# A two-layer kernel with a retention front end: a new list of loads, and another way to transpose two of its chunks

## The chip, the cores and the metric

The kernel runs on one core of a Trainium2 chip. The metric is the device time of one execution in microseconds (us); the median of six runs of the kernel before is 211.2 us (210.93 to 211.39). The core has TensorE (PE in the profile; PEld are its weight loads), VectorE (DVE), ScalarE (ACT), GpSimd (POOL) and SyncE (SP), which here does little but issue transfers. Each engine works through its own instructions in order, and engines meet at semaphores.

## The reference

Inputs q, k and v are float32 of shape 4 batches x 8 heads x 768 positions x 64. The first part is a linear attention with decay, the second a two-layer network with a squared relu; w_in is 512 x 2048 and w_out is 2048 x 512.

```python
gamma = 1.0 - 2.0 ** (-5.0 - np.arange(H))
for t in range(S):
    state = gamma[None, :, None, None] * state + np.einsum('bhd,bhe->bhde', k[:, :, t], v[:, :, t])
    y[:, :, t] = scale * np.einsum('bhd,bhde->bhe', q[:, :, t], state)
x = y.transpose(0, 2, 1, 3).reshape(B * S, H * D)     # 3072 tokens x 512
h = np.maximum(x @ w_in, 0.0)
out = h * h @ w_out                                   # 3072 x 512
```

## The kernel before

**Tiling.** The 3072 tokens are cut into 24 chunks of 128 (six a batch). Chunks 0 to 3 are handled as two pairs (`together`, `pair_visits`), named by their first chunk, pair 0 and pair 2. Each later chunk has a *visit* (`visit`, L714): values and state for chunk m, scores and sums for chunk n = m + 1. The decay is folded into scalings: v is multiplied by `vf` as it is cast to bf16, and the output by `yf` as it is written to `xt`, the input x of the network, transposed. `P` operations mask the scores, `S` operations add up the states, `Y` operations write x.

**Transposes.** The scores need q and k transposed (`qkT`). There are three ways, chosen by chunk number in `transpose` (L639): below NPE (from chunk 4), four 128x128 TensorE transposes each for k and q, and two evacuations; from NPE up to NTD, *flips*, which are 32 64x64 TensorE transposes inside the visit of an earlier chunk, into the bank of `yy`, and one evacuation on ACT (L635); from NTD on, one DMA transpose (`X`, L646), which SP issues. The visit that does the flips of chunk t is the one with n = t - 1, so it waits for the casts of k and q of chunk t as well.

**The network.** The first layer (`ffn1`, L804) works in blocks of 2, 2, 1, 1, 2, 2, 2, 4, 4, 4 chunks. Each group of matmuls fills one PSUM bank, ACT takes the relu (L827) and DVE squares (L832). The second layer (`ffn2`, L847) takes one chunk at a time and adds up in one bank over the four slices of w_out; at most two such accumulations are open at once. Four banks (`fps`) serve both layers and the 128x128 transposes.

**Weights.** w_in comes as i0 to i5: its first two quarters in halves (i0 and i1, i2 and i3, 512 KB each), the others whole (i4, i5, 1 MB). w_out comes as o0 to o3, 1 MB each. All land in float32 in four staging tiles `wst` and are cast to bf16 from there. In `weights` (L785) the tile is chosen by

```python
slot = (j if kind == "in" else 4 + j) % NWS
```

with NWS = 4 and j the quarter, so o0 uses the tile of i0 and i1, o1 that of i2 and i3, o2 that of i4, o3 that of i5, and each waits for the casts of what was there before.

**The order of the work.** Nothing is scheduled on the chip. A planner, `Plan.schedule`, places all operations with modelled lengths, earliest start first and then by priority, and the instructions are written out in that order. It also chooses the engine of an operation that could run on several (casts, evacuations), unless `HOME` names one, and `RANK` replaces a priority. The priority of a load is its place in `ORDER` (L233); loads are issued by SP. For loads the model keeps a ring of 198 outstanding descriptors, the time at which descriptors are made, and a pipe that moves bytes; it also models that TensorE's instructions are fetched in blocks of 256, and that a fetch makes one of the DMA engines late (`late`). TensorE's own priorities: the second layer's by F2LAG, the visits' by PACE, below which they go ahead of all else. Where the model leaves TensorE idle in the first 20 us, it puts in *fills*, matmuls of the identity with itself (L923), whose results are not used. `PRE` is a number of 1x1 matmuls ahead of everything.

Of the kernel before, what the change touches and what calls it, by code (L numbers as in the profile page):

```python
# [18 lines left out]
class Plan:  # L19
# [21 lines left out]
    def add(self, name, eng, dur, reads=(), writes=(), fn=None, prio=0.0, lat=0.0, bank=None, after=(), count=0):  # L41
# [17 lines left out]
        else:  # L59
            flex = True  # L60
        if name in HOME:
            eng = {HOME[name]: eng[HOME[name]]}
        prio = RANK.get(name, prio)
# [4 lines left out]
    def schedule(self, nbanks, max_open):  # L68
        ops = self.ops
        n = len(ops)  # L70
        users = [[] for _ in range(n)]
        left = [len(o["deps"]) for o in ops]
        for o in ops:
            for d in o["deps"]:
                users[d].append(o["i"])
        ready_at = [0.0] * n
        start = [None] * n
        end = [None] * n
        eng_free = {}
        pool = {}  # L80
        for o in ops:
            for e in o["eng"]:
                eng_free.setdefault(e, 0.0)
                pool.setdefault(e, set())
                if left[o["i"]] == 0:
                    pool[e].add(o["i"])
        if "PE" in eng_free:
            eng_free["PE"] = 0.06 * PRE
        bank_free = [0.0] * nbanks
        bank_of = {}  # L90
        open_groups = set()
        closed = {}
        pipe = made = 0.0
        late = []
        outstanding = {e: [] for e in eng_free}
        done = 0
        issued, edge, next_fetched, history, crossed = 2 * PRE, self.BLOCK0, 3.0, [], 0.0
        while done < n:
            best = None
            for eng, cand in pool.items():  # L100
                ef = eng_free[eng]
                for i in cand:
                    o = ops[i]
                    t = max(ef, ready_at[i])
                    b = o["bank"]
                    if b is not None and b[0] == "open":
                        if b[2] and len(open_groups) >= max_open:
                            continue
                        free = [x for x in bank_free if x is not None]
                        if not free:  # L110
                            continue
                        t = max(t, min(free))
                    key = (t, o["prio"], i)
                    if best is None or key < best[0]:
                        best = (key, i, eng)
            assert best is not None, "no operation can be placed"
            (t, _, _), i, eng = best
            o = ops[i]
            for e in o["eng"]:
                pool[e].discard(i)  # L120
            o["on"] = eng
            dur = o["eng"][eng]
            move = isinstance(dur, tuple)
            if move:
                gen, cost, n_desc, hold = dur
                out_ = outstanding[eng]
                while out_ and out_[0][0] <= t:
                    out_.pop(0)
                while sum(x[1] for x in out_) + n_desc > self.RING:
                    t = max(t, out_.pop(0)[0])  # L130
            start[i] = t
            before_open = list(bank_free)
            b = o["bank"]
            if b is not None and b[0] == "open":
                k = min((x, j) for j, x in enumerate(bank_free) if x is not None)[1]
                bank_free[k] = None
                bank_of[b[1]] = k
                if b[2]:
                    open_groups.add(b[1])
            if move:  # L140
                eng_free[eng] = t + hold
                if n_desc:
                    made = max(made, t + self.GEN_LATENCY) + gen
                    ready = made + 0.15
                else:
                    ready = t + hold + 0.5
                pipe = max(max(pipe, t + self.DMA_LATENCY) + cost, ready)
                late = [y for y in (max(max(y, t + self.DMA_LATENCY) + cost, ready) for y in late) if y > pipe + 0.05]
                end[i] = max([pipe] + late) + self.LAND
                out_.append((max([pipe] + late), n_desc))  # L150
                dur = hold
            else:
                if eng == "PE":
                    o["fill"] = 0
                    free = [(x, j) for j, x in enumerate(before_open) if x is not None and x <= max(eng_free[eng], WARM - WARMING)]
                    if WARM - WARMING < t < WARM + 1 and free:
                        o["fill"] = int(max(0.0, t - max(eng_free[eng], WARM - WARMING) - 0.1) / FILL)
                        o["fill_bank"] = min(free)[1]
                    issued += 2 * o["fill"]
                    before = issued  # L160
                    todo, per = 2 * o["count"], dur / max(1, 2 * o["count"])
                    now = t
                    while issued + todo > edge:
                        step = max(0, edge - issued)
                        now = max(now + step * per, next_fetched)
                        issued, todo = max(issued, edge), todo - step
                        ahead = next((y for x, y in reversed(history) if x <= edge - self.AHEAD), 0.0)
                        ahead = max(ahead, crossed)
                        crossed = now
                        edge += self.BLOCK  # L170
                        next_fetched = ahead + min(5.7, max(0.3, pipe - ahead)) + self.FETCH
                    issued += todo
                    dur = now + todo * per - t
                    history.append((issued, t + dur))
                    if any(before < x <= issued for x in range(self.BLOCK0 - self.AHEAD, issued + 1, self.BLOCK)):
                        late.append(max(pipe, t + 0.4) + 1.27)
                    o["dur"] = dur
                eng_free[eng] = t + dur
                end[i] = t + dur + o["lat"]
            if b is not None and b[0] == "close":  # L180
                closed.setdefault(b[1], []).append(end[i])
                if len(closed[b[1]]) == (b[2] if len(b) > 2 else 1):
                    bank_free[bank_of[b[1]]] = max(closed[b[1]])
                    open_groups.discard(b[1])
            if b is not None:
                o["bank_index"] = bank_of[b[1]]
            done += 1
            for u in users[i]:
                same = list(ops[u]["eng"]) == [eng] and not move
                ready_at[u] = max(ready_at[u], start[i] + dur if same else end[i] + self.HOP)  # L190
                left[u] -= 1
                if left[u] == 0:
                    for e in ops[u]["eng"]:
                        pool[e].add(u)
        self.start, self.end, self.on = start, end, [o["on"] for o in ops]
        return sorted(range(n), key=lambda i: (start[i], i))
# [10 lines left out]
WARM = 20.0  # L207
FILL = 0.215
WARMING = 18.4
PACE = 8  # L210
LEAD = 2
NPE = 7
NTD = 8
PRE = 0
WHALF = 2
WHALFD = (0.60, 1.47, 33, 0.6)
CVT = {'DVE': 0.69, 'POOL': 1.3}
TCAST = {'DVE': 0.43, 'ACT': 0.63, 'POOL': 0.78}
TEVAC = {'ACT': 0.6, 'DVE': 0.62}
NPAIR = 2  # L220
F2LAG = 3.0
F2WAIT = 4
LAST = [256, 128, 128]
CAST = {"k": {"DVE": 0.43, "ACT": 0.63, "POOL": 0.78}, "q": {"DVE": 0.43, "ACT": 0.63, "POOL": 0.78}}
# [2 lines left out]
WPRIO = {"in": -2.0, "out": 2.0}  # L227


HOME = {'cwin0.2': 'DVE'}  # L230
ROUND = []
RANK = {}
ORDER = (  # L233
    "q0 k0 v0 i0 k2 q2 v2 i1 i2 i3 k4 v4 i4 q4 i5 o0 k5 o1 q5 o2 v5 o3 k6 q6 v6 k7 q7 v7"
)


# [8 lines left out]
def kernel(  # L246
# [392 lines left out]
    def transpose(m):  # L639


        qkT, t = qkts[m % NQT], kq[m % NBF]
        if m < 2 * NPAIR or NPE <= m < NTD:
            return
        if m >= NPE:
            pl.add(f"X{m}", "SP", TURN, (f"bfk{m % NBF}", f"bfq{m % NBF}"), qkeys(m),  # L646
# [67 lines left out]
    def visit(m, n, t=None):  # L714
# [13 lines left out]
        def fn():  # L728
# [10 lines left out]
            if m is not None:  # L739
                nc.tensor.wait_ge(turn, turns[0])  # L740
                apply(m, 1)
        dur = 0.19 + 0.26 * ((m is not None) + (n is not None) + (t is not None))
        if n is None:
            dur += 0.2
        pl.add(f"V{'' if m is None else m}.{'' if n is None else n}", "PE", dur, reads, writes, fn,
               prio=-300 + n if m is None else -300 + m if m < PACE else (m - LEAD) * 8, lat=0.25,
               count=32 * ((m is not None) + (n is not None) + (t is not None)) + 1)
# [22 lines left out]
        if m is not None:  # L770
            g, u = divmod(m, 4)
            i = where(m)[1]
# [117 lines left out]
    for m in range(-1, NM):  # L890
        n = m + 1
        for x in range(0 if m < 0 else m + AHEAD, min(NM, m + AHEAD + 1)):
            prepare(x)
            transpose(x)
        t = m + 2 if NPE <= m + 2 < NTD else None
        if n < 2 * NPAIR:
# [60 lines left out]
```

## Time and profile before

| | |
|---|---|
| median of six runs | 211.2 us |
| profiled execution | 211.39 us |
| its span, first to last instruction | 209.6 us |
| mean granted TensorE clock | 0.984 |
| TensorE busy | 201.8 us (96%) |
| VectorE, ScalarE, GpSimd busy | 115.9, 87.9, 43.0 us |
| first layer, 640 matmuls (L822) | 93.0 us |
| second layer, 416 matmuls (L867) | 91.6 us |
| fills, 35 matmuls (L923) | 7.1 us |
| moved by DMA | 38.13 MB |
| DMA transposes | 16, each 5.0 us from issue to landing (median) |

Busy times of matmuls overlap, since they are pipelined and their ends are modelled, so the parts add up to more than TensorE's total. A line number names the line of the kernel that made the instruction; casts made through the helper `copy_on` appear under L404 (ACT), L406 (DVE) or L408 (POOL). The rows that issue transfers are marked SPq, and a transfer's own wait appears as "DMA tile<-tensor". Buffer numbers are left out of tile names, and the twin tiles of the pairs are part of `h`.

### The profile page before, as it was taken

The page shows a single profiled execution, that of the slowest core. Times are in us where ns is not written, and L with a number is a line of the kernel's source. Part 1 is how long each engine was busy: PE and PEld are TensorE (multiplying, and loading weights), DVE is VectorE, ACT ScalarE, POOL GpSimd, SP SyncE. Part 2 cuts the span into 40 slices and gives each one's busy share as a digit, 9 for nine tenths or more (in the row PEclk, how much of TensorE's full clock was granted, in tenths as well). Part 3 has the DMA queues.
Part 4 walks back from the last instruction along what each step waited for, and adds up shares of the span by engine and source line. Part 5 has one row for each costly group of instructions (what it writes and reads, how often), then busy time and mean ns, then how long its engine had stood idle before and what let it go on. Part 6 is the DMA issues. An engine that isn't in the chain of part 4 may idle for free.

```text
span 209.6 us, 6038 instructions
## 1 busy us (share of the span) xinstructions
PE 201.8 (96%) x2619; PEld 120.4 (57%) x2619; DVE 115.9 (55%) x252; ACT 87.9 (42%) x148; POOL 43.0 (21%) x71
## 2 busy tenths in 40 slices
PE   6789998999999999999999999999999999999994
PEld 4467886665665878666745444444444444444453
DVE  3667988785574686484825657567554432322100
ACT  8354576443441546234231365323533324534321
POOL 6634243233322121222311224021100000000000
PEclk9966999999999999999999999999999999999999
DMA  6999999999999999999998999999711011011022
GB/s 163 307 300 313 264 368 331 331 269 202 271 190 248 197 203 195 206 161 267 194 245 200 204 209 210 170 213 216 106 60 53 0 58 45 0 50 55 0 100 100
DMA packets 94586, 38.13 MB, mean 182 GB/s; under 512 B 79968, under 2 KB 88544, under 8 KB 94560
## 3 DMA queue, kind: packets, MB, share of 16 engines
q1 hardware_dynamic: 94416, 37.69, 84.0%
q8 instruction: 20, 0.33, 0.7%
q10 hardware_dynamic: 144, 0.07, 0.1%
q14 instruction: 6, 0.05, 0.1%
HBM read 27.26 MB, written 6.29 MB: 160 GB/s over the span
## 4 chain that ended last, share of the span: by engine, by line
PE 78%; DMA 11%; SPq 6%; POOL 1%; ACT 1%; issue 0%; DVE 0%; ACTq 0%
PE fps L867 39%; PE fps L822 33%; DMA qn<-in_q_dram 7%; DMA vn<-in_v_dram 4%; SPq L796 3%; SPq L423 2%; PE yy L673 2%; PE yy L688 1%; PE sc L699 1%; PE sc L710 1%; SPq L603 1%; POOL kqs L408 1%; POOL h L439 1%; ACT qkT L635 0%; PE fps L656 0%
## 5 line engine op out<-in xcount | busy, mean ns | idle before, releaser
L822 PE MATMUL fps<-xt,w_in 128*128 128x256 bf16 (+2 forms) x640 | 93.0, 296 | 0.1
L867 PE MATMUL fps<-w_out,h 128*128 128x512 bf16 (+2 forms) x416 | 91.6, 363 | 0.0
L827 ACT ACTIVATE h<-fps 128x512 bf16<-128x512 f32 x96 | 57.2, 596 | 68.4 <-PE fps L822 66.0
L822 PEld LDWEIGHTS <-w_in 128*128 128x128 bf16 x640 | 57.2, 98 | 30.0 <-issue 0.4
L832 DVE TENSOR_TENSOR h<-h 128x512 bf16<-128x512 bf16 x96 | 42.3, 451 | 47.4 <-ACT h L827 47.2
L867 PEld LDWEIGHTS <-h 128*128 128x128 bf16 x416 | 37.9, 98 | 37.1
L875 ACT ACTIVATE osb<-fps 128x512 f32<-128x512 f32 (+2 forms) x26 | 14.7, 564 | 35.7 <-PE fps L867 35.7
L408 POOL CAST kqs<-kn 128x512 bf16<-128x512 f32 x20 | 12.6, 629 | 48.1 <-DMA kn<-in_k_dram 43.4
L775 DVE TENSOR_TENSOR xt<-yy,yf 128x512 bf16<-128x512 f32 x20 | 13.7, 686 | 15.0 <-PE yy L688 13.9
L408 POOL CAST kqs<-qn 128x512 bf16<-128x512 f32 x20 | 14.2, 712 | 31.8 <-DMA qn<-in_q_dram 31.8
L614 DVE TENSOR_TENSOR vs<-vn,vf 128x512 bf16<-128x512 f32 x20 | 14.4, 718 | 5.8 <-DMA vn<-in_v_dram 5.8
L766 DVE TENSOR_TENSOR state<-sc,state 128x256 bf16<-128x256 f32 x33 | 13.8, 419 | 0.5
L753 DVE TENSOR_TENSOR pt<-sc,cmask 128x512 bf16<-128x512 f32 x20 | 13.6, 681 | 0.3 <-PE sc L710 0.3
L688 PE MATMUL yy<-qkT,state 64*64 64x64 bf16 x296 | 10.0, 198 | 0.2
L923 PE MATMUL fps<-ident 128*128 128x256 bf16 x35 | 7.1, 357 | 1.7 <-POOL ident L339 1.7
L673 PEld LDWEIGHTS <-vs 64*64 64x64 bf16 x320 | 4.2, 107 | 6.7 <-issue 6.6
L688 PEld LDWEIGHTS <-state 64*64 64x64 bf16 x296 | 6.2, 107 | 0.4 <-PE yy L688 0.4
L673 PE MATMUL yy<-pt,vs 64*64 64x64 bf16 x320 | 6.4, 198 | 0.0
L699 PE MATMUL sc<-qkT 64*64 64x64 bf16 x320 | 6.2, 194 | 0.0
L710 PE MATMUL sc<-vs,kqs 64*64 64x64 bf16 x288 | 6.2, 193 | 0.0
L406 DVE CAST w_out<-wst 128x512 bf16<-128x512 f32 x8 | 4.7, 632 | 2.7 <-DMA wst<-in_moe_w_out_dram 2.6
L408 POOL CAST w_in<-wst 128x512 bf16<-128x512 f32 x6 | 4.2, 696 | 8.9 <-DMA wst<-in_moe_w_in_dram 8.9
(65 smaller groups left out, 88.3 us busy)
## 6 DMA issues: line engine op xcount, KB each, us to landing
out_dram<-osb SPq DMA_DIRECT2D x23, 256.0 KB, 2.9
kn<-in_k_dram SPq DMA_DIRECT2D x20, 256.0 KB, 5.0
vn<-in_v_dram SPq DMA_DIRECT2D x20, 256.0 KB, 5.1
qn<-in_q_dram SPq DMA_DIRECT2D x20, 256.0 KB, 4.9
wst<-in_moe_w_out_dram SPq DMA_DIRECT2D x4, 1024.0 KB, 10.5
wst<-in_moe_w_in_dram SPq DMA_DIRECT2D x4, 512.0 KB, 8.5
wst<-in_moe_w_in_dram SPq DMA_DIRECT2D x2, 1024.0 KB, 8.1
qn<-in_q_dram SPq DMA_DIRECT2D x2, 512.0 KB, 6.1
```

The costliest lines, as they stand in the source:

```text
L408: nc.gpsimd.tensor_copy(o, t)
L614: lambda: nc.vector.tensor_tensor(out=o[:], in0=t.rearrange("s (h d) -> s h d", h=H), in1=vf[:, i, :, None].to_broadcast([P, H, D]), op=AL ...
L673: nc.tensor.matmul(yy[L * c : L * c + L, sub, p * L : p * L + L], lhsT=vs[r, 4 * a + j, :], rhs=pt[r, a, j, :], start=(p == 0), stop=True, ...
L688: nc.tensor.matmul(yy[L * c : L * c + L, sub, p * L : p * L + L], lhsT=st[r, j, :], rhs=qkT[r, 1, j, sub * L : sub * L + L], start=False, ...
L753: lambda: nc.vector.tensor_tensor(out=pt[:], in0=sc[:, :, 0:256].rearrange("s g (p t) -> s g p t", p=NJ), in1=cmask[:, None, None, :].to_b ...
L766: f = lambda cc=cc, j1=j1, j0=j0: nc.vector.tensor_tensor(out=sts[j1][:], in0=cc, in1=sts[j0][:], op=ALU.add)
L775: lambda: nc.vector.tensor_tensor(out=xt[:, :, u * C : u * C + C].rearrange("s p (g t) -> s g p t", g=2), in0=yy[:, :, 0:256].rearrange("s ...
L822: nc.tensor.matmul(ps[:, u * n : u * n + n], lhsT=w_in_bf[j][:, cb, c * P : (c + 1) * P], rhs=xt[:, cb, cols], start=(cb == 0), stop=(cb = ...
L827: nc.scalar.activation(h2[:, f0 : f0 + per, cols], ps[:].rearrange("p (u n) -> p u n", u=per), AF.Relu)
L832: nc.vector.tensor_mul(hv, hv, hv)
L867: nc.tensor.matmul(ps[:, 0:w], lhsT=h2[:, fb, u * C : u * C + C], rhs=w_out_bf[j][:, c, ns], start=(fb == 0), stop=(fb == NFB - 1))
L875: lambda o1=o1, slot=slot, ns=ns, w=w: nc.scalar.activation(osbs[slot][:, ns], fps[o1["op"]["bank_index"]][:, 0:w], AF.Copy),
```

## The change

It does four things. In the planner's model of loads, a fetch of instructions is now placed ahead of those loads whose descriptors aren't made yet, and these loads are then made later, with the work that waits for them; before, it went behind the whole pipe. A new `ORDER` puts k0 ahead of q0, loads q and k of the second pair before the first half slice of w_in and v after it, interleaves the slices of w_out with those of w_in, and puts q5, q6 and q7 ahead of k5. NPE goes from 7 to 6 and NTD from 8 to 7: chunk 6 is transposed by flips and no longer by 128x128 transposes, chunk 7 by DMA and no longer by flips. And the constants that the planner works with are others: 20 matmuls of 1x1 at the start, F2LAG 4, PACE 5, a longer modelled visit, an engine named for 27 casts and evacuations, and one evacuation of the first pair put ahead.

```diff
@@ Plan.schedule, a load
+                moves.append((made if n_desc else t, pipe, cost, ready, t, i, out_))
                 pipe = max(max(pipe, t + self.DMA_LATENCY) + cost, ready)
...
-                out_.append((max([pipe] + late), n_desc))
+                out_.append([max([pipe] + late), n_desc, i])
@@ Plan.schedule, a fetch of instructions
-                        late.append(max(pipe, t + 0.4) + 1.27)
+                        behind = [x for x in moves if x[0] > t + 0.4]
+                        y = max(behind[0][1] if behind else pipe, t + 0.4) + 1.27
+                        for _, _, cost, ready, t0, k, out_ in behind:
+                            y = max(max(y, t0 + self.DMA_LATENCY) + cost, ready)
+                            if y + self.LAND > end[k]:
+                                end[k] = y + self.LAND
...
+                                for u in users[k]:
+                                    ready_at[u] = max(ready_at[u], end[k] + self.HOP)
+                        late.append(y)
@@ constants
-PACE = 8
+PACE = 5
-NPE = 7
-NTD = 8
-PRE = 0
+NPE = 6
+NTD = 7
+PRE = 20
-F2LAG = 3.0
+F2LAG = 4.0
-HOME = {'cwin0.2': 'DVE'}
+HOME = {'cq2.1': 'POOL', 'Eq2.0': 'DVE', 'cq0.1': 'ACT', 'cwout3.3': 'ACT', 'cwin2.0': 'DVE', 'cwin0.0': 'ACT', 'ck2.0': 'ACT', 'ck5': 'DVE', 'Eq4': 'DVE', 'Eq0.1': 'ACT', 'cq4': 'ACT', 'cwin1.2': 'ACT', 'ck6': 'DVE', 'Ek0.0': 'DVE', 'cwout2.3': 'DVE', 'cwin1.0': 'ACT', 'cwin3.2': 'DVE', 'Ek4': 'ACT', 'cwout0.3': 'DVE', 'cq0.0': 'DVE', 'ck4': 'POOL', 'cwin5.2': 'ACT', 'cwout0.1': 'DVE', 'cwout3.1': 'DVE', 'cwout1.3': 'DVE', 'cwout1.0': 'DVE', 'cwout0.2': 'DVE'}
-RANK = {}
+RANK = {'Ek0.0': -98.1}
 ORDER = (
-    "q0 k0 v0 i0 k2 q2 v2 i1 i2 i3 k4 v4 i4 q4 i5 o0 k5 o1 q5 o2 v5 o3 k6 q6 v6 k7 q7 v7"
+    "k0 q0 v0 q2 k2 i0 v2 o0 k4 i1 o1 i2 q4 o2 i3 o3 i4 v4 i5 q5 q6 q7 k5 v5 v6 k6 k7 v7"
 )
@@ visit
-        dur = 0.19 + 0.26 * ((m is not None) + (n is not None) + (t is not None))
+        dur = 0.22 + 0.28 * ((m is not None) + (n is not None) + (t is not None))
```

More of the change, by code (lines that the diff above doesn't have):

```diff
@@ L94, in schedule @@
         late = []
+        moves = []
         outstanding = {e: [] for e in eng_free}
@@ L175, in schedule @@
                     if any(before < x <= issued for x in range(self.BLOCK0 - self.AHEAD, issued + 1, self.BLOCK)):
-                        late.append(max(pipe, t + 0.4) + 1.27)
+                        behind = [x for x in moves if x[0] > t + 0.4]
[4 more added lines that the diff above has]
+                                end[k] = y + self.LAND
+                                for x in out_:
+                                    if x[2] == k:
+                                        x[0] = max(x[0], y)
+                                for u in users[k]:
+                                    ready_at[u] = max(ready_at[u], end[k] + self.HOP)
+                        late.append(y)
                     o["dur"] = dur
```

## The prediction

> **What bounds the kernel now.** I read the page first, to see whether TensorE or the transfers set the pace: the row of engines, TensorE's busy tenths, its granted clock, and the transfers' share.
>
> ```profile
> span 209.6 us, 6038 instructions
> PE 201.8 (96%) x2619; PEld 120.4 (57%) x2619; DVE 115.9 (55%) x252; ACT 87.9 (42%) x148; POOL 43.0 (21%) x71
> PE   6789998999999999999999999999999999999994
> PEclk9966999999999999999999999999999999999999
> DMA  6999999999999999999998999999711011011022
> ```
>
> TensorE is full from the tenth slice (47 us) to the tail. The other engines are half idle, and the loads fill the DMA engines long past 50 us. So the change can win or lose only where TensorE waits for data, early. The chain that ended last says the same: ahead of 40 us it runs through loads, after it through matmuls. Four of its rows:
>
> ```profile
> 7.60 8.05 DMA vn<-in_v_dram
> 29.93 9.32 DMA qn<-in_q_dram
> 84.36 0.87 PE fps L822 x8
> 85.23 0.86 PE fps L867 x4
> ```
>
> The last two give the price of a group: 0.87 us for the first layer of a pair (8 matmuls), 0.86 us for the second layer (4 matmuls). The timeline then shows when weights land, by the cast that waits for them, and when TensorE runs dry (columns: start, length, engine, line, operation, and in brackets the idle time before it):
>
> ```profile
> 31.36 2.79 PE L822 MATMUL fps<-xt,w_in 128*128 128x256 bf16 x24
> 34.73 1.05 PE L822 MATMUL fps<-xt,w_in 128*128 128x256 bf16 x8
> 36.28 0.40 PE L656 MATMUL fps<-ident,kqs 128*128 128x128 bf16 x4 [0.50 <-POOL kqs L408]
> ...
> 46.01 1.17 DVE L406 CAST w_out<-wst 128x512 bf16<-128x512 f32 x2 [0.43 <-DMA wst<-in_moe_w_out_dram]
> ...
> 47.10 1.03 PE L867 MATMUL fps<-w_out,h 128*128 128x512 bf16 x4
> ```
>
> Slice o3 of w_out lands at 46.0, its casts end at 47.2. Counting groups from the timeline: by 47.1 all first-layer work of chunks 0 to 4 is done, and of the second layer the six groups that two open accumulations allow without o3. So until 47.1 TensorE uses up whatever lands; behind that stand the ten second-layer groups of chunks 2 to 4 (8.6 us), and it doesn't run dry again. **The last landing of w_out, with what TensorE has finished by then, sets the end.** A second narrow place is chunk 7:
>
> ```profile
> 58.96 2.59 SPq L647 DMA_TRANSPOSE qkT<-kqs  x1
> 65.35 0.32 PE L673 MATMUL yy<-pt,vs 64*64 64x64 bf16 x16
> 66.18 0.69 DVE L775 TENSOR_TENSOR xt<-yy,yf 128x512 bf16<-128x512 f32 x1 [2.58 <-PE yy L688]
> 67.76 1.91 PE L822 MATMUL fps<-xt,w_in 128*128 128x256 bf16 x16
> 76.28 1.90 PE L867 MATMUL fps<-w_out,h 128*128 128x512 bf16 x8
> ```
>
> Chunk 7's x is ready at 66.9 and used at 67.8; only two groups (1.7 us, those at 76.28) were left as other work. TensorE could go without chunks 6 and 7 until 69.5.
>
> **What the Trainium skill says.** "Runtime: NRT & Kernel Launch", Instruction fetch mechanics: instructions arrive in 16 KiB blocks of 256 through the sequencer's own DMA queue. The trace agrees: the instruction queue has 20 packets in 0.33 MB, 16.5 KB each, and 2 x 2619 TensorE instructions are 20.5 blocks. "DMA: Bandwidth & Descriptors", Queues, rings and completion order: all rows share the same 16 engines and take turns. It agrees where it can be seen: slice i1 lands 2.9 us after the transfer ahead of it, its like take 1.5, so a disturbance is worth 1.4 us. "TensorE: Matmul & The Clock Gate", Part 1: half clock until a window of about 3.4 us was busy. Here the clock is 0.50 from 14 to 18 us and 1.00 from 20, and eight 256-column matmuls take 1.92 us at 15.9 but 1.05 at 20.6.
>
> **The change, part by part.**
>
> *List of loads.* Landings now: k0 6.8, v0 8.7, i0 10.2, k2 11.95, q2 13.8, v2 15.7, i1 18.6, i2 20.1, i3 21.9, i4 26.7, i5 30.5, o0 34.25, o1 38.15, o2 42.1, v5 43.2, o3 46.0. Differences price a load: pair 1.85, half w_in slice 1.5, 1 MB slice 2.75, single 1.05. The new list names o0 before i1, but o0 shares a staging tile with i0 and i1 and is issued after their casts; o1 likewise after i2 and i3, o2 after i4, o3 after i5. SP issues what is ready, so I expect: k0 q0 v0 q2 k2 i0 v2 k4 i1 i2 q4 i3 i4 v4 i5 o0 q5 o1 q6 o2 o3, then the rest. Summed with these prices, the same 1.4 us disturbance (put at k4) and 1.0 us (o0 now takes 3.75): k2 12.3, i0 13.8, v2 15.7, k4 18.1, i1 19.6, i2 21.1, i3 23.7, i4 26.4, v4 27.5, i5 30.2, o0 34.0, o1 37.8, o2 41.6, **o3 44.4**. Two single loads stand ahead of o3 in place of three: that is 1.05 of the 1.6 us; the rest is rounding and spacing.
>
> *Half a slice within the second pair.* i0 lands 3.6 us later, at 13.8, cast by 14.5; x of the first pair is ready only at 15.0 (now 14.34+0.69), so nothing waits. In return q2 and k2 land some 1.5 to 1.8 us earlier, so the scores of pair 2 leave the path of v2: its x comes near 20.2 in place of 23.7.
>
> *TensorE, walked through with these landings* (a w_in half's casts 0.7 us, a 1 MB slice's 0.9 to 1.2): first group at 15.0 to 16.9, cold, as now. From 20.3 three groups to 22.9, i2's two to 24.6, i3's two to 26.4, transposes to 26.8, i4's four from 27.3 to 30.8, chunk 4's visits, i5's four to 35.3, chunk 4's four groups (0.89 each) to 38.9, o0's two to 40.6, transposes and o1's two to 42.6, o2's two to 44.6, then a wait for o3's casts until **45.6**. Now the same point is at 47.1: 1.5 us. Against it, the chunk 5 visit (0.37) and one transpose group (0.22) are then still to do, and one pair is gone (next edit): 1.35 us stay.
>
> *Chunk 6 by flips, chunk 7 by DMA transpose.* Two groups of four TensorE transposes leave (0.22 each, from 48.97 for the quartet at 49.05 against its follower at 49.27): 0.44 us, counted above. The 32 flips move from chunk 7 to chunk 6, net zero; two evacuations (0.4 to 0.6 us each on DVE or ACT) leave and the 1.0 us one stays. Added: one DMA transpose, 2.0 to 2.6 us on SP and 4.2 to 6.4 us to landing. Queued behind it on SP are the loads of chunk 8 and stores; those delayed by up to 2.6 us are q8 and v8, and so chunk 8's own transpose, which releases the visit at 65.35. I take 1.0 us of that, as k8 and q8 are 2.5 us apart now[...]; bounds 0 and 2.6. Chunk 7's x then comes near 67.9, and TensorE, ahead by 1.35, has other work until 68.1. Free, just; without that cover, 1 us per us. Also new: chunk 5's visit waits for k6, which lands near 49.6 behind k5, v5 and v6; 8.6 us of other work cover it, if it stands ahead in TensorE's list.
>
> *Twenty 1x1 matmuls at the start.* No row shows this form. Even at 0.2 us each (an isolated 64x64) they end by 4.5 us, before the first transposes at 5.5; at the lower end they hide in the 1.7 us before the identity is made. Taken as 0. They move the fetch boundaries by 40 instructions: -1.4 to +1.4 us on some load, taken as 0.
>
> *Pinned casts, priorities, the later second layer, the visit's modelled length.* These move work between engines that are half idle, or change the order inside a full TensorE: 0, with the order risk below.
>
> Sum: 211.39 (the profiled execution; span 209.6 and 1.8 around it) less 1.35, plus 0.25 for small waits in the new list such as the 0.5 us shown above, is 210.3; the median of the runs is 0.2 lower, 211.2, so 210.1.
>
> **Rivals.**
> - *Only the transposes are saved:* q7 also slips in ahead of o3, or a fetch hits an o slice; o3 stays at 45.5 to 46. Gain 0.2 to 0.5, about 210.8. For it: SP passes over a slice that isn't ready.
> - *Given back at chunk 7:* its x comes at 69.2 to 69.6, and TensorE stands until then: 211.2, no change. For it: the slack was 1.7 us; against: the flips used to hold up chunk 6's visit too.
> - *Slower:* TensorE runs a list in order, and the first visit that needs chunk 7's DMA transpose stands in it. k7 lands some 6 single loads after o3, near 50.7, and is cast by 51.4, so the transpose lands at 56 to 60; if the list puts that visit (now at 57.65) ahead of the landing, all of the backlog waits behind it, and each us costs one. From 1.35 us late it is a loss; at 3 us, 212.8. For it: the added SP hold and the chain through k6. Against: of TensorE's waits between 22.5 and 70 us the trace names only one, 0.5 us.
> - *Clock:* full clock comes one window later, 22.2 us in place of 18.8; half speed from 20.3 then loses about 1 us, and the walk's waits near 27 and 45 (0.5 and 1.0) take it up. 210.2; not decisive.
>
> **How the numbers follow.** Forecast with the clock case 0.38; only the transposes 0.18 (0.10 of it beyond the bound); given back 0.07; slower 0.37, because several in-order waits are new and each needs the new list to be right within a us. A measurement here tells some 0.2% (0.4 us) from no change. Faster: 0.38 + 0.10 = 0.48; same 0.15; slower 0.37. The likeliest case runs from 209.2 to 210.6; with the fetch's 1.4 us as a gain 209.0 at the low end, and the slower case with 3 us of lateness at 212.8 at the high end.
>
> **What would show it.** Right: the last w_out casts start near 44.4, TensorE's first stretch without other work ends at 45.6, pair 2's x before 21, no TensorE idle over 0.5 us between 50 and 70. Wrong: w_out casts at 46 or later; a TensorE wait on chunk 7's transpose or on k6; first-layer groups at 215 ns a matmul after 20 us.

## The result: 0.2 per cent slower, and the profile after

The changed kernel takes 211.5 us (median of 31 runs, 210.68 to 214.88), the kernel before 211.1 us (67 runs, 210.45 to 212.31) on the same chip. The ratio is 1.0022, with a 95% interval of 1.0012 to 1.0032: a small loss where 210.1 us was forecast. The profiled execution that came with the result is one of two slow ones (214.88 and 214.37 us), which the ratio leaves out, so the lines below are of a repeat of the changed kernel (`again_look`), whose profiled execution took 211.58 us. In the changed kernel line numbers are 13 higher (first layer L835, second layer L880, DMA transposes L660, the scores of a visit L712).

The page of the repeat, the same rows as shown of before (busy times; busy tenths and granted clock in 40 slices):

```profile
span 209.8 us, 6053 instructions
PE 200.3 (95%) x2627; PEld 119.7 (57%) x2627; DVE 115.2 (55%) x252; ACT 88.9 (42%) x150; POOL 40.0 (19%) x67
PE   7786999999998999999999999999999999999994
PEclk9999799999999999999999999999999999999999
DMA  6999999999999999999989999399931110110212
```

TensorE's busy time fell from 201.8 to 200.3 us and the span did not: there is new idle time. It shows as a 6 in the fourth slice (16 to 21 us) and an 8 in the thirteenth (63 to 68 us).

First, did the loads come as forecast? The timeline of the repeat, casts of the last two slices of w_out (start, length, engine, line, operation; in brackets the idle time before):

```profile
40.77 0.63 ACT L417 ACTIVATE w_out<-wst 128x512 bf16<-128x512 f32 x1 [0.29 <-DMA wst<-in_moe_w_out_dram]
43.56 1.15 ACT L417 ACTIVATE w_out<-wst 128x512 bf16<-128x512 f32 x2 [0.44 <-DMA wst<-in_moe_w_out_dram]
```

o2 comes at 40.8 (before 42.1, forecast 41.6) and o3 at 43.6 (before 46.0, forecast 44.4), better than forecast. TensorE's timeline has no wait for it:

```profile
42.33 4.05 PE L880 MATMUL fps<-w_out,h 128*128 128x512 bf16 x18
46.64 0.39 PE L669 MATMUL fps<-ident,kqs 128*128 128x128 bf16 x4
```

So the gain was made in this execution. To see what became of it I added up the work that TensorE had issued by a given time (every layer group at its 0.87 us, a visit at the 0.67 us that it takes where nothing waits, fills left out; where a trace lacks a matmul's record, its weight load counts), and took the difference to the kernel before; the 0.44 us of chunk 6's transposes, which TensorE no longer does, count as done. The lead over the kernel before, in us, in one trace of each kernel (a step of 0.2 is one matmul):

| kernel | 60 us | 66 | 80 | 90 | 120 | 200 |
|---|---|---|---|---|---|---|
| changed (the repeat) | 1.25 | 0.23 | 0.22 | -0.21 | -0.22 | -0.21 |
| changed (another trace, `again`) | 0.07 | 0.00 | -0.11 | -0.87 | -0.65 | -0.87 |
| before with the new list alone | 1.36 | 1.31 | 1.08 | 0.87 | 0.21 | 0.00 |
| changed, fills and one group moved | 1.80 | 1.53 | 0.98 | 0.33 | 0.44 | 0.44 |
| changed, fills and six groups moved | 1.80 | 1.75 | 1.41 | 1.53 | 1.74 | 1.31 |

The last three, and the other trace of the changed kernel, are explained below. At 60 us the changed kernel is ahead by 1.25 us in the repeat, about the 1.35 forecast. By 66 us 1.0 us of it is gone, in one place:

```profile
55.68 1.60 SPq L893 DMA_DIRECT2D out_dram<-osb  x1
55.85 0.61 POOL L421 CAST kqs<-qn 128x512 bf16<-128x512 f32 x1 [1.87 <-DMA qn<-in_q_dram]
...
58.60 2.26 SPq L660 DMA_TRANSPOSE qkT<-kqs  x1
...
63.27 0.32 PE L686 MATMUL yy<-pt,vs 64*64 64x64 bf16 x16
...
64.52 0.32 PE L712 MATMUL sc<-qkT 64*64 64x64 bf16 x16 [0.87 <-DMA qkT<-kqs]
64.96 1.90 PE L880 MATMUL fps<-w_out,h 128*128 128x512 bf16 x8
```

This is the visit V7.8 (values of chunk 7, scores of chunk 8). TensorE reaches it at 63.27 and stops until chunk 8's DMA transpose has landed, at 64.5; the second-layer work that follows at 64.96 was ready, but stands behind the visit in TensorE's list. In the kernel before the same visit began at 65.35 and waited for nothing: its transpose, issued at 58.96, was there. Its scores, and the time from issue to landing of that transpose, in the kernel before; then the time to landing in the repeat:

```profile
65.56 0.30 PE L699 MATMUL sc<-qkT 64*64 64x64 bf16 x16
DMA to landing us min/median/max: 4.9/4.9/4.9
```

```profile
DMA to landing us min/median/max: 5.9/5.9/5.9
```

So it landed at 63.9 there, 1.7 us ahead of its use. TensorE comes 2.1 us sooner now (1.25 of lead, the rest because one group of work less stands ahead of the visit). The transpose is issued 0.4 us sooner, but takes longer and lands 0.6 us later, at 64.5. With 1.7 us in hand, that leaves the scores 1.0 us of waiting. The POOL cast that it needs ends at 56.46, but SyncE works through its own list, and the store of 55.68 to 57.28, which waits for the second layer's output, and two loads stand ahead of it. Later it happens again at V10.11, for chunk 11's transpose (issued 77.85; before 76.16):

```profile
77.85 2.71 SPq L660 DMA_TRANSPOSE qkT<-kqs  x1
...
83.12 0.32 PE L712 MATMUL sc<-qkT 64*64 64x64 bf16 x16 [0.48 <-DMA qkT<-kqs]
```

The second piece of idle time is early. TensorE around 18 us in the repeat:

```profile
15.50 1.05 PE L835 MATMUL fps<-xt,w_in 128*128 128x256 bf16 x8
...
18.53 0.60 PE L512 MATMUL fps<-h 64*64 64x64 bf16 x32 [1.77 <-POOL h L452]
...
20.99 3.16 PE L835 MATMUL fps<-xt,w_in 128*128 128x256 bf16 x16
```

POOL's share of v2's scaling starts at 16.9 (before 15.7, forecast 15.7), and pair 2's state waits for it. Windows of TensorE's time in the repeat and then in the kernel before (window, sum, PE busy, granted clock, DMA share, GB/s):

```profile
16.00:18.00 2.00, 0.76 (x7) 1.00 1.08 325
18.00:20.00 2.00, 1.40 (x60) 1.00 1.18 302
20.00:22.00 2.00, 1.94 (x33) 0.54 1.11 324
```

```profile
16.00:18.00 2.00, 2.00 (x22) 0.50 1.10 346
18.00:20.00 2.00, 1.96 (x82) 0.69 1.18 314
20.00:22.00 2.00, 1.75 (x44) 1.00 0.94 164
```

The half-clock stretch, in the kernel before over the transposes and the first group (12.4 to 19.2 us), is now at 20.2 to 23.6 us, where it has first-layer groups.

### The profile page after: what moved, and what is told of

The parts are those of the page before. It is cut to its first block, busy times and chain, and to the rows that moved or that the text cites. A ratio compares the mean times of both kernels' runs of the same rounds, so it can differ in the third digit from the quotient of the medians.

```text
span 213.1 us, 6053 instructions
## 1 busy us (share of the span) xinstructions
PE 201.2 (94%) x2627; PEld 119.5 (56%) x2627; DVE 114.7 (54%) x252; ACT 88.1 (41%) x150; POOL 40.4 (19%) x67
## 4 chain that ended last, share of the span: by engine, by line
PE 65%; DMA 21%; SPq 9%; DVE 2%; POOL 1%; issue 1%; ACT 0%
PE fps L880 31%; PE fps L835 28%; SPq L616 7%; DMA qkT<-kqs 5%; DMA kn<-in_k_dram 5%; DMA qn<-in_q_dram 4%; DMA wst<-in_moe_w_in_dram 3%; DMA vn<-in_v_dram 3%; SPq L436 2%; PE yy L686 2%; PE yy L701 1%; PE sc L712 1%; PE sc L723 1%; SPq L809 1%; DVE h L558 1%
## 5 line engine op out<-in xcount | busy, mean ns | idle before, releaser
L835 PE MATMUL fps<-xt,w_in 128*128 128x256 bf16 (+2 forms) x640 | 90.9, 296 | 0.3 <-POOL w_in L421 0.2
L880 PE MATMUL fps<-w_out,h 128*128 128x512 bf16 (+2 forms) x416 | 89.3, 363 | 1.4 <-POOL w_out L421 1.1
L840 ACT ACTIVATE h<-fps 128x512 bf16<-128x512 f32 x96 | 56.4, 596 | 53.8 <-PE fps L835 53.8
L835 PEld LDWEIGHTS <-w_in 128*128 128x128 bf16 x640 | 57.2, 99 | 29.1 <-POOL w_in L421 0.4
L880 PEld LDWEIGHTS <-h 128*128 128x128 bf16 x416 | 38.1, 98 | 41.1 <-issue 1.9
L421 POOL CAST kqs<-kn 128x512 bf16<-128x512 f32 x18 | 11.8, 656 | 55.6 <-DMA kn<-in_k_dram 48.0
L627 DVE TENSOR_TENSOR vs<-vn,vf 128x512 bf16<-128x512 f32 x20 | 13.7, 686 | 10.5 <-DMA vn<-in_v_dram 10.4
L421 POOL CAST kqs<-qn 128x512 bf16<-128x512 f32 x19 | 12.5, 660 | 29.6 <-DMA qn<-in_q_dram 29.3
L712 PE MATMUL sc<-qkT 64*64 64x64 bf16 x320 | 6.2, 194 | 1.2 <-DMA qkT<-kqs 1.2
L936 PE MATMUL fps<-ident 128*128 128x256 bf16 x31 | 6.4, 356 | 0.3 <-POOL ident L352 0.3
```

The lines of the kernel that those rows point to most:

```text
L421: nc.gpsimd.tensor_copy(o, t)
L627: lambda: nc.vector.tensor_tensor(out=o[:], in0=t.rearrange("s (h d) -> s h d", h=H), in1=vf[:, i, :, None].to_broadcast([P, H, D]), op=AL ...
L835: nc.tensor.matmul(ps[:, u * n : u * n + n], lhsT=w_in_bf[j][:, cb, c * P : (c + 1) * P], rhs=xt[:, cb, cols], start=(cb == 0), stop=(cb = ...
L840: nc.scalar.activation(h2[:, f0 : f0 + per, cols], ps[:].rearrange("p (u n) -> p u n", u=per), AF.Relu)
L880: nc.tensor.matmul(ps[:, 0:w], lhsT=h2[:, fb, u * C : u * C + C], rhs=w_out_bf[j][:, c, ns], start=(fb == 0), stop=(fb == NFB - 1))
```

## The experiments

All ratios are against the kernel before, run beside them on the same chip.

**Parts of the change alone.** The list of loads without anything else; the transposes without anything else; and the change with its transposes undone.

```diff
(list_alone: kernel before)
 ORDER = (
-    "q0 k0 v0 i0 k2 q2 v2 i1 ...
+    "k0 q0 v0 q2 k2 i0 v2 o0 k4 i1 ...
(transposes_alone: kernel before)
-NPE = 7
-NTD = 8
+NPE = 6
+NTD = 7
(transposes_undone: changed kernel)
-NPE = 6
-NTD = 7
+NPE = 7
+NTD = 8
```

> The kernel before with the new list of loads and nothing else of the change (old model, old transposes, old constants). Theory A: 0.993 to 0.996 of before, 0.9 to 1.5 us faster. Theory B: 1.000 to 1.005.

> The kernel before with chunk 6 by flips and chunk 7 by DMA transpose, nothing else changed. Theory A: 1.003 to 1.007 of before, since chunk 7's DMA transpose and the wait for k6 cost 0.7 to 1.5 us. Theory B: 0.998 to 1.000, since 0.44 us of TensorE transposes leave and nothing else moves.

> The changed kernel with the two transposes undone (NPE 7, NTD 8), list and constants as changed. Theory A: 0.993 to 0.997 of before. Theory B: 1.002 to 1.005, as the changed kernel or 0.4 us worse.

Measured: list alone 1.0026 (1.0006 to 1.0047), transposes alone 1.0100 (1.0058 to 1.0143), transposes undone 1.0020 (0.9998 to 1.0043). No single part carries the gain, and the transposes alone lose 1.9 us. Why the change without its transposes is no faster is open: in its one trace v2 is late and TensorE is 0.5 us behind the kernel before at 60 us. The waits of TensorE from 26 to 120 us with the transposes alone (engine and line, releaser, us in total, times, longest):

```profile
PE sc L699 <- DMA qkT<-kqs: 1.5, 1, 1.5
PE fps L822 <- POOL w_in L408: 0.7, 2, 0.4
```

One wait of 1.5 us at V7.8, where the repeat has 0.9; without the new list there is no lead to pay it from. Here chunk 8's transpose is late: it lands at 66.2, in the kernel before at 63.9. A second trace of the list alone shows where that part loses its lead.

> The list alone once more, for a second trace: its runs fall into two groups, spans of 208.3 to 208.8 and of 210.1 to 211.2 us, and the first trace is of the faster one. Theory C (half clock): a run of the slower group has half clock between 18 and 26 us and TensorE starts 2 us behind. Theory D (waits for transposes and casts in in-order queues): the clock is 1.0 and TensorE stands 1 us or more at visits between 50 and 90 us. Should it be of the faster group again, it tells nothing new.

It took 211.31 us. Its waits from 26 to 120 us:

```profile
PE sc L699 <- DMA qkT<-kqs: 0.5, 2, 0.3
PE fps L822 <- DVE xt L775: 0.3, 1, 0.3
```

With chunk 7 still done by flips, V7.8 is passed without a wait, and of the lead of 1.3 us 0.9 is left at 110 us. There V15.16 waits for chunk 16's transpose, and the first layer of the next four chunks for its x; in the table the lead drops from 0.87 to 0.21. Chunk 16's transpose was issued at 104.31 there and at 104.16 in the kernel before: a TensorE that is 0.9 us ahead doesn't get its transposes any sooner. The first trace of the list alone, of a run of 210.40 us, still had 0.9 us of its lead at 200 us: this list gets through in some executions.

**The changed kernel again**, for a trace other than that of 214.88 us.

> The changed kernel once more, for a trace without disturbance. Theory A (the list of loads wins, the two other transposes give it back): the casts of o3 start near 44.4 us, and TensorE stands for 1 to 2 us between 52 and 70 us, at the visits of chunk 5 and chunk 7. Theory B (the list itself brings nothing): o3's casts start at 45.5 us or later and TensorE waits for the slices of w_out before that, about 1 us or more.

> The changed kernel a third time. Theory C: half clock between 18 and 26 us, TensorE 1.5 to 2 us behind the kernel before at 28 us. Theory D: a wait of 0.6 to 1.2 us for a DMA transpose at one of the visits of chunks 7 to 10, or for chunk 5's masks.

212.09 and 211.58 us; the second is the one shown above. The first is another case. Its granted clock, and the scores of V7.8:

```profile
PEclk9997599999999999999999999999999999999999
64.84 0.30 PE L712 MATMUL sc<-qkT 64*64 64x64 bf16 x16
```

The clock was half from 18.7 to 25.6 us, twice as long as in the repeat, and at 30 us TensorE was 1.7 us behind the kernel before (the repeat 0.4). The early landings came to nothing here: at 60 us it is 0.1 us ahead. V7.8 waits for nothing in this trace; V10.11 waits 0.6 us. So the loss at V7.8 is shown for the repeat, and the gain at the front was not there in every run.

**The early hole and the clock.** Twelve more fills ahead of the products of pair 2 keep TensorE busy while v2 is awaited.

```diff
+    for o in pl.ops:
+        if o["name"] == "B2":
+            o["fill"] += 12
```

> The changed kernel with 12 more fills ahead of the second pair's sums, where TensorE stood from 16.8 to 18.7 us. Theory C (the hole drops the clock to half at 20 to 26 us and that costs the gain): most runs keep a granted clock of 1.0, and 0.994 to 0.998 of before. Theory D: 1.001 to 1.003, as the changed kernel, whatever the clock does.

1.0008 (0.9996 to 1.0020). The half-clock stretch behind the hole is gone, and the mean clock of the span was at full (0.998 or more) in all 18 runs, against 7 of 32 of the changed kernel. The gain of some 0.3 us is not certain: the intervals overlap, and among the changed kernel's runs those with the lower clock were not the slower ones (medians 211.26 us for the lowest, 211.50 for full clock). V7.8 still waited 0.6 us.

Two runs on why v2 is late: without the twenty 1x1 matmuls, and with i0 back ahead of the second pair.

```diff
(nopre: changed kernel)
-            for _ in range(PRE):
+            for _ in range(0):
(i0_early: changed kernel; "ahead" moves one operation of the finished list)
+    ahead("ldwin0", "ldq2")
```

> The changed kernel's own list without the twenty 1x1 matmuls at the start, so that TensorE's blocks of instructions are fetched 40 instructions later. Theory G (the first fetch falls into v2 and makes it land at 17.0 in place of 15.7 us, which makes the hole in TensorE at 16.8): v2 lands near 15.7, the hole closes, and the time is 0.998 to 1.001 of before. Otherwise 1.001 to 1.003, with v2 at 17.

> The changed kernel with one part of its list undone: the first half slice of w_in (i0) goes back in SP's queue ahead of q2, as it stood ahead of the second pair before. Theory H (i0 in the middle of the pair holds back the issue of v2 until the first fetch of instructions stands ahead of it): v2 lands near 15.7 in place of 17.05, the hole in TensorE shrinks from 1.9 us to below 1, more runs keep full clock, 0.998 to 1.001 of before. If only the number of bytes ahead of v2 counts: v2 at 17, 1.001 to 1.003.

Without the 1x1 matmuls: 1.0051 (1.0037 to 1.0065), v2 as late as before that edit. With i0 first: 1.0041 (1.0026 to 1.0057); v2 was issued at 7.56, as early as in the kernel before (7.60), and its cast still began at 16.9. Neither the matmuls nor v2's place behind i0 is the cause alone. In the traces v2's cast begins near 15.5 (15.7 in the kernel before) or near 17.0, and nowhere between: 15.5 in three of the four traces of the new list without the other edits, near 17.0 in those of the changed kernel. The instruction block fetched nearby does not sort them cleanly: in the twelve traces in which it starts before 14 us, v2 is late in all; in the eight in which it starts later, in two. What decides it stays open; the step is about 1.4 us, the size that the prediction gave to a disturbance and set to nothing.

**How much the last slice of w_out is worth.** o3 put behind v5, as it was in the kernel before.

```diff
+    behind("ldwout3", "ldv5")
```

> The changed kernel with slice o3 moved back in SP's queue behind q7, k5 and v5, so that it lands at 46 to 47 us again, as in the kernel before, and TensorE waits for it near 45 us. Theory F (the forecast: the last slice of w_out sets the end): 2 to 3 us slower than the changed kernel, 1.012 to 1.016 of before. Theory E (the lead that the early slice gives is lost anyway at chunk 7's and chunk 10's visits, which wait for DMA transposes that come when they come): at most 0.8 us slower than the changed kernel, 1.002 to 1.006 of before.

1.0133 (1.0102 to 1.0164), which is 2.3 us more than the changed kernel. TensorE in this run:

```profile
47.53 1.15 ACT L417 ACTIVATE w_out<-wst 128x512 bf16<-128x512 f32 x2 [4.54 <-DMA wst<-in_moe_w_out_dram]
...
48.49 1.02 PE L880 MATMUL fps<-w_out,h 128*128 128x512 bf16 x4 [2.61 <-POOL w_out L421]
```

A landing 4.0 us later costs a wait of 2.6 us, and most of that reaches the end. So the prediction's bound is real in this direction: lateness here costs nearly in full. Earliness doesn't pay in the same way.

**Taking the waits away, first singly.** Work put ahead of V7.8 and V10.11, and a store and a load put behind the transposes on SyncE's list, the second with and without the fills.

```diff
(cover)
+    ahead("P5", "cv7")
+    ahead("S5.0", "cv7")
+    ahead("F2.4.3", "V7.8")
+    ahead("F2.6.2", "V10.11")
+    ahead("F2.6.3", "V10.11")
(sp_order; sp_warm is the same with the 12 fills)
+    behind("st2", "X8")
+    behind("ldv12", "X11")
```

> The changed kernel with five operations moved ahead in its list and nothing else: chunk 5's masks and first state ahead of chunk 7's v on VectorE; one second-layer group ahead of chunk 7's visit and two ahead of chunk 10's, so that the DMA transposes of chunks 8 and 11 have 0.9 and 1.7 us more. Theory D: 0.994 to 0.998 of before. Theory C: 1.001 to 1.003, as the changed kernel.

> The changed kernel with two moves in SP's queue: the store of chunk 2 goes behind chunk 8's DMA transpose, and the load of v12 behind chunk 11's. These transposes are ready at 56.5 and 76.0 us and were issued at 58.6 and 77.9. Theory E: the waits of 1.0 and 0.6 us at the visits of chunks 7 and 10 shrink or go, 0.995 to 0.999 of before, the rest being half clock. Theory F: no change from the changed kernel, 1.001 to 1.003.

> Both moves in SP's queue and the 12 fills that held the clock. Theory E with half clock as the second cost: 0.993 to 0.997 of before, the forecast's gain. Theory F: 1.000 to 1.002, as with the fills alone.

cover 1.0035 (1.0018 to 1.0051), sp_order 1.0044 (1.0029 to 1.0058), sp_warm 1.0002 (0.9987 to 1.0018). In cover both waits are gone, but its trace, with half clock from 19.0 to 25.8 us, has no lead at 60 us that could be lost; and a new wait of 1.1 us stands ahead of the first layer of chunks 10 and 11, for their x. In sp_order V10.11 no longer waits, V7.8 still does, and V12.13 starts to. Here the fills do tell: sp_order and sp_warm differ by 0.4 per cent, with intervals apart. Whether by the clock is not shown: the five runs of sp_order at full clock were no faster than the others (medians 212.4 and 211.7 us).

> The changed kernel with the 12 fills and one second-layer group ahead of chunk 7's visit, nothing else moved. Theory E (the lead is lost at this visit): its wait of 0.7 to 1.0 us goes, TensorE is 0.9 us or more ahead of the kernel before at 68 us, and the time is 0.994 to 0.998 of before. If the wait only moves on to the next visits or to the first layer: 0.999 to 1.001, as with the fills alone.

> The kernel before with the new list of loads alone and 8 fills ahead of the second pair's sums. Theory C (half clock makes the slower half of the runs of the list alone): all runs at full clock, and 0.995 to 0.998 of before. Otherwise the runs stay split, 0.999 to 1.003.

The fills and one group (F2.4.3) ahead of V7.8: 1.0001 (0.9986 to 1.0016). V7.8 is passed, the lead at 66 us is 1.5 us instead of 0.2, and then it is lost at V8.9 and V10.11 (the fourth row of the table):

```profile
PE sc L712 <- DMA qkT<-kqs: 1.0, 2, 0.6
```

The new list with 8 fills: 0.9999 (0.9980 to 1.0017). Five of its 14 runs still had the lower clock, and they were the slower ones (medians 211.6 and 210.6 us).

**Taking them all away.** What was open now: can the lead be kept at all, or do the visits' inputs set a pace that takes back any lead? One kernel moves a group of work ahead of nearly every visit at which one of the earlier traces had waited; another does the same for the list alone; the last makes such moves in the kernel before.

```diff
(v78_more: changed kernel with 12 fills)
+    ahead("F2.4.3", "V7.8")
+    ahead("F1.4.10", "V8.9")
+    ahead("F1.5.6", "V10.11")
+    ahead("F1.5.8", "V10.11")
+    ahead("F2.11.1", "V15.16")
+    ahead("F2.11.3", "F1.7.0")
(list_cover: new list with 8 fills)
+    ahead("F2.10.1", "V15.16")
+    ahead("F2.10.3", "F1.7.0")
(before_cover: kernel before)
+    ahead("F2.5.0", "V7.8")
+    ahead("F1.4.4", "V8.9")
+    ahead("F2.6.0", "V10.11")
+    ahead("F1.5.10", "V10.11")
+    ahead("F2.11.1", "V15.16")
```

> Theory P (TensorE's gain of 1.5 us at 50 us is given back because the visits' inputs, the DMA transposes on SyncE's queue, come at a pace of their own, at which the kernel before arrives just in time): with the fills and second-layer work ahead of V7.8 and V8.9, and first- and second-layer work ahead of V10.11, V15.16 and the first layer of pair 7, each of these waits shrinks to under 0.3 us where it stands, and the run shows whether the list after that has any wait left. If nothing waits later, the lead of about 1.0 us that the run with V7.8 alone had at 80 us is kept to the end: 0.994 to 0.997 of the kernel before. Theory R (the lead can't be kept, since a delayed visit delays the next chunk's state, its output and the x of its pair): new waits for x or for a transpose behind the moved ones, 0.999 to 1.002.

> The new list alone with 8 fills ahead of the second pair's products, and one second-layer group each ahead of V15.16 and of the first layer of pair 7, the two places where the list alone lost 0.9 us of a lead of 1.0 at 110 us. Theory P: both waits gone, the lead at 120 us about 1.0 where the list with fills has 0.4, 0.9955 to 0.9975 of the kernel before. Theory R: the waits move to a later visit (V16.17, V17.18), 0.999 to 1.001.

> The kernel before with the same kind of moves (one group of TensorE work each ahead of V7.8, V8.9 and V15.16, two ahead of V10.11) and nothing of the change. Theory P: the kernel before has no lead that these visits take back (it waits 0.2 us at V10.11 and nowhere else there), so it gains at most that: 0.999 to 1.001. Rival M (the moves alone made the last run fast, with the change or without): 0.994 to 0.997.

v78_more takes 209.8 us, 0.9950 (0.9934 to 0.9966): faster than both kernels. list_cover takes 210.25 us, 0.9975 (0.9958 to 0.9992). before_cover takes 211.24 us, 1.0006 (0.9996 to 1.0015): the moves are worth nothing without the change. With the same fills and the clock full in every run, the changed kernel goes from 1.0008 (warm) to 0.9950 by the six moves, with intervals far apart. The six moves without the fills were not run. The page of v78_more:

```profile
span 207.9 us, 6053 instructions
PE   7788999999999999999999999999999999999994
PEclk9999999999999999999999999999999999999999
```

TensorE is full from the fifth slice on. Chunk 11's transpose is issued no earlier than in the changed kernel (78.25 and 77.85), but where V10.11 would have waited, five groups now run first, and the visit starts at 82.76 without a wait:

```profile
78.25 1.83 SPq L660 DMA_TRANSPOSE qkT<-kqs  x1
78.29 4.54 PE L835 MATMUL fps<-xt,w_in 128*128 128x256 bf16 x40
82.76 0.32 PE L686 MATMUL yy<-pt,vs 64*64 64x64 bf16 x16
```

The lead of 1.8 us at 60 us is 1.3 to 1.7 for the rest of the span (last row of the table). So the lead is not taken back by a pace; where the clock holds, it was lost by the order in which TensorE's list met it.

## Why the prediction was wrong

**Right.** The landings: every slice of w_out within 0.9 us of its forecast, on the early side. The order in which SyncE issues. The price of one of the transposes' edits: TensorE's part is gone. The size of the gain at the front in the repeat: 1.25 us at 60 us, 1.35 forecast; in `again`, with the longer half clock, it was 0.1. The sums of the parts too, once the waits are covered: list_cover is 0.87 us below the kernel before where the list's share of the forecast was 0.91 (1.35 less 0.44), and v78_more another 0.45 us below list_cover, where the transposes' share was 0.44. The intervals are some 0.35 us to either side on each, so this agreement is closer than it had to be.

**The step that failed** is the sentence that behind 47.1 us TensorE "doesn't run dry again", and with it that the last landing of w_out "sets the end". That was read from the kernel before, and there it holds: TensorE comes to V7.8 at 65.35, to V10.11 at 82.47, and finds its transposes landed or 0.2 us away. What the view of waits could not show is how close this was. The prediction says that chunk 8's transpose "releases the visit at 65.35"; in the trace it landed at 63.9, and was used 1.7 us later. The lead of 1.25 us alone would have fitted into this margin. TensorE came 2.1 us sooner, with one group less ahead of the visit, and the landing came 0.6 us later; what is over, 1.0 us, became a wait. The prediction did follow this transpose, but only to chunk 7's x ("near 67.9"), and held against it the work left "until 68.1", as if any of it could run first. A list in order can use only what stands ahead of the visit; the groups at 64.96 stood behind it. The rival "Slower" named this very mechanism, but put it at chunk 7's transpose and let it begin with a late landing. For chunk 8's the larger part is TensorE's being early (2.1 us), the smaller the late landing (0.6 us).

**Chunk 7 "free, just."** For chunk 7 that was true: the repeat has no wait for its transpose, and of the "1.0 us" of delay to chunk 8's there are 0.6. On the old list of loads the same edit isn't free at all: transposes alone are 1.9 us slower, and their trace has chunk 8's transpose 2.4 us later, within the stated bound of 2.6, and 1.5 us of wait at V7.8.

**v2 at 15.7, pair 2's x at 20.2.** v2's scaling began at 16.9 and the x of pair 2 came at 22.0 in the repeat (22.9 in `again`, 23.7 in the kernel before). The term that failed is the fetch shift "taken as 0"; v2's delay of 1.2 us is within its stated bounds of 1.4, though its cause isn't shown to be a fetch.

**Clock "not decisive".** The stretch of half clock moved as that rival said. Its price was put at about 1 us, hidden by waits. In `again`, with the longer stretch, TensorE was 1.3 us further behind at 30 us than in the repeat, and at 60 us there was no lead: nothing hid it there. Over all runs the fills take the ratio from 1.0022 to 1.0008, which may be nothing; in one other pair of kernels they are worth 0.4 per cent. One reading is that the lead is lost only once, to half clock or at the visits, so that a fill which saves the clock leaves it to the visits; no run was made to test that. In the medians the clock is a smaller part of the miss than the visits, and not a settled one.

**Twenty 1x1 matmuls** are not harmful: without them the ratio was 1.0051.

## What to carry to other kernels

A slack of zero waits in a profile isn't slack: before counting a gain at the front, go through the in-order list for each later point at which the bounding engine meets another's result, and write down how early that result was. What exceeds such a margin can be lost there, unless work is moved ahead of that point. The margin is of one trace, and landings move too. Here six groups moved turned 1.0008 into 0.9950, with the twelve fills in both. And look at more than one trace before saying where a gain went. Test a candidate for "what sets the end" in both directions: making it later cost nearly in full here, where there was no slack, and says nothing about what making it earlier brings.

## What the runs showed of the hardware

- The Trainium skill, "TensorE: Matmul & The Clock Gate", Part 1, has the clock halve after at least one idle window of about 3.4 us. In the repeat less idle time stood ahead of it: 1.8 us without a matmul, with TensorE 0.76 us busy of the 2 us from 16 and 1.40 of the next 2, was followed by half clock from 20.2 to 23.6 us. Such a hole is not always followed by it: in the trace of sp_order TensorE was busy 0.85 and 1.28 us in the same windows, and the clock stayed full; 7 of the changed kernel's 32 runs had full clock over the span. With twelve fills in the hole (2.00 and 1.40 in v78_more) it stayed full in all 52 runs of the four kernels that have them.
- A DMA transpose of one chunk's k and q takes 4.6 us from issue to landing in the repeat (median of the 15 whose landing is recorded; 5.0 in the kernel before), and SyncE stays with it for 1.3 to 4.1 us, so each is also a delay to what is queued behind it there.
- The landing of v2 has two values, near 15.5 and near 17.0 us, with the same bytes ahead of it; what picks between them is open.
